# Turning the MLP's input with block transposes and a trip through DRAM instead of on PE, two modulation vectors from 512 KB loads, and a new instruction order, in a planned one-core transformer block

## The chip, the cores and the metric

The kernel runs on one core of one Trainium2 chip. The metric is device time in microseconds of one execution; smaller is better. The engines are PE (matrix multiply; PEld is its weight load), DVE (vector), ACT (activation), POOL (general purpose) and SP, which issues the DMAs here.

## The reference, cut to what matters

`x` has 2048 rows of 512 values. Everything is float32.

```python
mod = (silu(c) @ w_mod).reshape(1, 6, 1, 512)
sa, ca, ga, sb, cb, gb = six rows of mod
h = layernorm(x) * (1 + ca) + sa
x = x + ga * A(h)                # 32 heads of 16, linear attention
h = layernorm(x) * (1 + cb) + sb
x = x + gb * B(h)

def A(x):
    q, k, v = heads of x @ wqkv
    phi(t) = concat(softmax(t @ w_phi), softmax(-(t @ w_phi)))   # per head
    o = phi(q) @ (phi(k).T @ v) / (phi(q) @ sum(phi(k)) + 1e-6)
    return o @ wo

def B(x):
    h = gelu(layernorm(x) @ w1)
    hs = concat of the four quarters of h, shifted by +1, -1, +2, -2 rows
    x1 = x + hs @ w2
    return x1 + gelu(layernorm(x1) @ w3) @ w4     # 512 -> 1376 -> 512
```

## The kernel before

**Precision.** A float32 product that must be exact enough is made of three matmuls in PE's float32r format: every operand is split into a high part, which ACT makes by a copy with rounding, and a low part, which DVE or POOL makes as the difference (`hi_lo`). `three` lists the matmuls high by high, high by low, low by high. An operand that is not split goes through PE as plain float32, and the profile counts each such matmul as two records.

**Stages.** Rows are worked on in 8 chunks of 256 (two tiles of 128).

1. Start: `w_phi` is folded into the K and the Q weights (`load_folded`: each weight is cut into sixteen 128 x 128 blocks, and each block is one matmul of `raw` by a block-diagonal `bd`; four blocks, a row of 128 x 512, make one fold, so there are four folds for K and four for Q). `mod_cols` makes `sa` and `1 + ca` as columns, from two of the six parts of `w_mod`: each part is loaded in four 256 KB pieces, scaled by silu(c) and summed (`acc`), and then summed over partitions by matmuls with one column of ones.
2. K, V and Q for each chunk (`h_chunk`, `k_feat`, `v_feat`, `q_feat`, `kv_add`): the normalised rows are turned by PE transposes (`pt<-const,xn`), scaled and split into `hh`. The Q features are stored to DRAM.
3. Attention output and first half of B for each chunk (`phase_a`, `mix`): Q features come back (`e`), get their denominators on DVE and POOL, DVE turns them in 32 x 32 blocks (`turn`, `pT`), PE multiplies by the key-value matrix (`num`, `pp<-pT,const`), `oT` is multiplied by `wo`, then two layernorms, PE transposes (`pt<-const,n`), `w1`, gelu, the shift, `w2`. The rows `x1` (tile `h`) and `x2` go to DRAM.
4. The MLP for each chunk (`phase_b`): `x1` is loaded (`xl`), normalised to `nb`, turned by eight PE transposes (`pt<-const,nb`), split into two `bH` tiles; `up_pair(j)` makes 256 of the 1376 hidden values (`pa<-bH,w`), gelu and the seven combinations of a fast 2 x 2 block product (`gg`); `down(j)` multiplies them by seven prepared blocks of `w4`; `out` and `d` add the pieces to `gb * x1 + x2` and store. POOL prepares `w4` (`raw`, `tw`, `w`) as stage 3 ends.

**What sets the order.** No instruction is issued where the code stands. Every helper records an `Op` with an engine, a cost, tiles read and written and, for some, alternative engines. `Plan.order` then places them one at a time: on every engine it takes, among the instructions that could start within `BIAS["window"]` ns of the earliest, the one with the lowest `o.prio`, which is its number in the code plus `PRIO[group]`; `PICK` and `BIAS` decide between engines; `CAP` limits how many tiles of a name live at once. The groups are named by `plan.at`: `k3` the keys of tile 3, `q3` its queries, `b2` the MLP of chunk 2, `l4` the input of tile 4 to it, and so on. The result is one fixed sequence for each engine, and each engine works through it strictly in order. All DMAs are issued by SP, and each waits until the one eight before it has landed.

```python
o.prio = o.i + PRIO.get(o.group, 0), o.i
...
s, o = min(((s, o) for s, o in cand if s <= first + window), key=lambda z: z[1].prio)
```

Of the kernel before, what the change touches and what calls it, by code (L numbers as in the profile page):

```python
# [9 lines left out]
FR = mybir.dt.float32r  # L10
AF = mybir.ActivationFunctionType
OP = mybir.AluOpType
# [3 lines left out]
P = 128  # L16
# [19 lines left out]
        "s4": ("ke", "qe", "e", "ez", "pT", "gf", "gg", "bH", "za", "tw"),  # L36
        "s2": ("raw", "mod", "acc", "bd", "xl", "xn", "h", "n", "xb", "xc", "gb", "vv", "kvs", "qt", "sg", "gl", "uu", "nb"),
# [3 lines left out]
CAP = {"acc": 19, "bH": 5, "bd": 5, "const": 71, "dram": 17, "e": 3, "ez": 19, "gb": 19, "gf": 10, "gg": 17, "gl":  # L41
# [4 lines left out]

PRIO = {"b0": -185, "b2": -126, "b3": -374, "b4": -71, "b5": 677, "b7": -111, "d0": 184, "d1": -4, "d2": -248, "d3":
# [25 lines left out]
PICK = {"b0": 1500, "b1": 3000, "b2": -3000, "b3": 3000, "b4": 2000, "b5": -1000, "b6": 1000, "b7": 500, "d0":  # L73
# [1113 lines left out]
```

## Time and profile before

| | before |
|---|---|
| median of 3 runs | 594.35 us (594.02 to 595.15) |
| the profiled execution | 594.79 us, of which its span is 593.0 us |
| PE busy | 568.4 us, 96% of the span |
| DVE, ACT, POOL busy | 417.0, 325.8, 350.1 us |
| HBM traffic | 47.76 MB read, 20.97 MB written |

In rows of the profile, `out<-in` are the program's tile names without their numbers, `x16` is a count of records, and what stands after a bar is the busy time in us, the mean ns of one, and the idle time of the engine just before. A row of the timeline or of the chain of waits has start and length in us. Rows by stretch give for each engine its busy time within the stretch, then the granted share of the PE clock, the share of the DMA engines and GB/s.

### The profile page before, as it was taken

Reading aid. Unit: us, or ns where it says so; the run is one execution under the profiler, and the core shown is the slowest. Engines: PE = TensorE matmul, PEld = TensorE weight load, DVE = VectorE, ACT = ScalarE, POOL = GpSimd, SP = SyncE. Lnnn points to the kernel's source line nnn. Section 1 sums busy time; section 2 is a strip of 40 time slices with the busy share of each in tenths; the row PEclk is TensorE's granted clock in tenths of the full one; section 3 lists DMA queues with packets and bytes.
Section 4 is the critical chain, followed back from the end, with each engine's and each line's share of the span. In section 5 each row is a group of like instructions: output and inputs, shape, how many; then the busy total and the mean of one; then the engine's idle time right before and its main releaser. Section 6 shows DMA issues by size and latency. Waiting matters only on the chain.

```text
span 593.0 us, 11872 instructions
## 1 busy us (share of the span) xinstructions
PE 568.4 (96%) x4548; PEld 512.4 (86%) x4548; DVE 417.0 (70%) x830; ACT 325.8 (55%) x699; POOL 350.1 (59%) x293
## 2 busy tenths in 40 slices
PE   4799999999998799999999999999999999999996
PEld 4588888888887478888888899999999999999996
DVE  5567999697399998898863555568475757556644
ACT  4889986683424575555668755545353435243332
POOL 2779998578998487757859699973321210310031
PEclk9799999999999799999999999999999999999999
DMA  8935524320344435534363532240404040303020
GB/s 278 300 110 177 179 80 166 114 88 2 125 143 170 181 129 178 196 104 172 117 212 107 178 103 90 67 137 25 144 1 143 2 125 1 107 1 107 2 90 37
DMA packets 33865, 69.51 MB, mean 117 GB/s; under 512 B 4144, under 2 KB 4784, under 8 KB 33808
## 3 DMA queue, kind: packets, MB, share of 16 engines
q1 hardware_dynamic: 33808, 68.75, 34.9%
q8 instruction: 36, 0.59, 0.4%
q14 instruction: 21, 0.17, 0.1%
HBM read 47.76 MB, written 20.97 MB: 116 GB/s over the span
## 4 chain that ended last, share of the span: by engine, by line
PE 78%; POOL 7%; DMA 5%; DVE 5%; issue 2%; ACT 2%; SPq 1%; POOLq 0%; DVEq 0%
PE pp L460 52%; PE pa L460 22%; PE pt L469 3%; DMA e<-dram 2%; POOL w L411 2%; POOL raw L411 2%; DMA mod<-in_wmod 2%; PE kva L460 1%; POOL tw L411 1%; DMA raw<-in_w 1%; DVE pp L429 1%; SPq L440 1%; DVE pT L727 1%; POOL ez L411 1%; ACT n L392 1%
## 5 line engine op out<-in xcount | busy, mean ns | idle before, releaser
L460 PE MATMUL pa<-bH,w 128*128 128x256 f32 (+1 forms) x1056 | 130.8, 279 | 0.0
L460 PEld LDWEIGHTS pa<-bH,w 128*128 128x128 f32 (+1 forms) x1056 | 126.0, 186 | 0.2
L460 PE MATMUL pp<-w,gg 128*128 128x256 f32 x840 | 107.6, 280 | 0.6 <-POOL w L411 0.6
L460 PEld LDWEIGHTS pp<-w,gg 128*128 128x128 f32 x840 | 102.7, 188 | 2.0 <-POOL w L411 1.0
L460 PE MATMUL pp<-w,hh 128*128 128x512 f32 x384 | 93.9, 401 | 2.9 <-ACT hh L392 2.9
L460 PEld LDWEIGHTS pp<-w,hh 128*128 128x128 f32 x384 | 72.1, 191 | 19.3 <-ACT hh L392 3.0
L409 DVE TENSOR_TENSOR sg<-sg,pa 128x128 f32<-128x128 f32 x80 | 22.6, 282 | 64.3 <-ACT pa L392 64.3
L411 POOL TENSOR_TENSOR w<-raw,w 128x512 fp32r<-128x512 f32 (+3 forms) x40 | 46.1, 1163 | 20.5 <-ACT w L392 19.1
L460 PE MATMUL pp<-w,oT 128*128 128x512 f32 x192 | 49.4, 407 | 2.5 <-DVE oT L409 1.7
L392 ACT ACTIVATE sg<-pa 128x128 f32<-128x128 f32 x40 | 11.1, 276 | 73.5 <-PE pa L460 70.4
L411 POOL TENSOR_TENSOR xb<-xb,gb 128x512 f32<-128x512 f32 x10 | 13.8, 1382 | 63.5 <-DMA xb<-dram 56.2
L460 PE MATMUL pp<-w,sh 128*128 128x512 f32 x192 | 50.5, 401 | 0.1
L460 PEld LDWEIGHTS pa<-nT,w 128*128 128x128 f32 x384 | 47.4, 188 | 2.5 <-issue 1.2
L460 PE MATMUL pp<-hh,w 128*128 128x256 f32 x384 | 48.9, 285 | 0.0
L460 PE MATMUL pa<-nT,w 128*128 128x256 f32 x384 | 48.7, 283 | 0.0
L460 PEld LDWEIGHTS pp<-hh,w 128*128 128x128 f32 x384 | 46.6, 189 | 2.2 <-issue 1.1
L460 PEld LDWEIGHTS pp<-w,oT 128*128 128x128 f32 x192 | 37.1, 195 | 11.9 <-DVE oT L409 2.5
L392 ACT ACTIVATE gg<-pa 128x384 fp32r<-128x384 f32 x40 | 19.7, 492 | 48.1 <-DVE sg L409 47.2
L411 POOL TENSOR_TENSOR ke<-ke,k 128x1024 f32<-128x1024 f32 x16 | 30.9, 1941 | 21.0 <-DVE k L437 7.2
L411 POOL TENSOR_TENSOR ez<-e,const 128x1024 f32<-128x1024 f32 x16 | 38.2, 2398 | 6.8 <-DMA e<-dram 6.1
L460 PEld LDWEIGHTS pp<-w,sh 128*128 128x128 f32 x192 | 34.2, 188 | 8.8 <-issue 1.6
L535 POOL TENSOR_TENSOR rs<-rs,const 128x1 f32<-128x1 f32 x18 | 10.2, 575 | 51.7 <-DVE rs L421 51.5
(142 smaller groups left out, 1114.3 us busy)
## 6 DMA issues: line engine op xcount, KB each, us to landing
xl<-in_x SPq DMA_DIRECT2D x32, 256.0 KB, 3.5
dram<-qe SPq DMA_DIRECT2D x16, 512.0 KB, 2.9
e<-dram SPq DMA_DIRECT2D x16, 512.0 KB, 4.8
raw<-in_w SPq DMA_DIRECT2D x26, 256.0 KB, 3.4
mod<-in_wmod SPq DMA_DIRECT2D x24, 256.0 KB, 4.6
dram<-xl SPq DMA_DIRECT2D x16, 256.0 KB, 2.0
xc<-dram SPq DMA_DIRECT2D x16, 256.0 KB, 4.7
dram<-h SPq DMA_DIRECT2D x16, 256.0 KB, 2.1
```

What stands on the lines that cost most here:

```text
L392: nc.scalar.activation(o(), i(), func, **kw)
L409: dve = ("DVE", 71 + 1.04 * o.n + 90 * (isps(a) and isps(b)), lambda: nc.vector.tensor_tensor(o(), a(), b(), op=op))
L411: pool = ("Pool", cost, lambda: nc.gpsimd.tensor_tensor(o(), a(), b(), op=op))
L429: nc.vector.scalar_tensor_tensor(o(), a(), get(s), b(), op0=op0, op1=op1, **kw)
L440: plan.op("SP", 475, lambda: nc.sync.dma_start(o(), get(src)), [o], [src] if isinstance(src, V) else [], lat=nbytes / 360., after=after)
L460: nc.tensor.matmul(o(), a(), b(), start=s, stop=e, **kw)
L469: nc.tensor.transpose(o(), i(), ident())
L535: plan.op("Pool", 550, lambda: nc.gpsimd.tensor_tensor(r(), v(), mhalf[:, 0:1](), op=OP.pow), [r], [v, mhalf])
L727: plan.op("DVE", 71 + 1.04 * o.n, lambda: nc.vector.transpose(o(), i()), [o], [i])
```

## The change

- **Start.** The small loads of `c`, of the constants and of `w_phi` are issued by ACT (`load_act`). Three groups of four matmuls of a 128 x 128 tile of ones by itself are put on PE (`warm`). The weights to be folded have tiles of their own (`rk`) and the order takes all eight folds ahead of the first projection.
- **Modulation columns.** The two parts come in four loads of 512 KB that hold both. The first part goes as before. For the second, the raw weights are PE's stationary operand and silu(c) is the single moving column, so that the four pieces are summed in PSUM.
- **MLP input.** `layernorm(..., mixed=True)` writes its result with columns reordered in groups of 32; DVE turns 32 x 32 blocks (`yt`); the tile is stored to a DRAM tile `yd`; four DMAs for each chunk (`load_turned`) load it in 512-byte pieces so that it lies turned in `bL`. ACT copies the high part to `bH`, and DVE or POOL leaves the low part in `bL`. In `up`, the low part is read by PE as 8 pieces of 32 columns that lie 128 columns apart.
- **Order.** `PRIO`, `PICK`, `CAP` and `BIAS` are other numbers throughout, and one rule of the plan's PE clock is altered.

```diff
-CAP = {"acc": 19, "bH": 5, "bd": 5, "const": 71, ...
+CAP = {"acc": 6, "bH": 4, "bL": 13, "bd": 9, "const": 71, ...
-PRIO = {"b0": -185, "b2": -126, "b3": -374, ...
+PRIO = {"b0": -200, "b1": 213, "b2": 706, "b3": 93, ...
-BIAS = {"DVE": 6037, "Pool": 3164, "window": 7, ...
+BIAS = {"DVE": 1908, "Pool": -296, "window": 7, ...
...
-    load(cc, c_d, 2048)
+    load_act(cc, c_d, 2600)
     cst = T("const", [P, 2 * P])
-    load(cst, cst_d, 131072)
+    load_act(cst, cst_d, 3000)
...
+    plan.at("warm")
+    for _ in range(3):
+        p = T("pp", [P, NK, P])
+        mms([(p[:, k, :], ones, ones, True, True) for k in range(NK)], [p], [ones])
...
-    def mod_cols(j):
-        acc = mod_acc(j)
-        p = T("pp", [P, NK])
-        mms([(p[:, k:k + 1], acc[:, k * P:(k + 1) * P], ones[:, 0:1], k == 0, k == NK - 1) for k in range(NK)],
+    def mod_cols():
+
+        acc, p = T("acc"), T("pp", [P, 2, NK])
+        for k in range(NK):
+            raw = T("mod2", [P, 2, D])
+            load(raw, wmod_d[k * P:(k + 1) * P, :2 * D].rearrange("p (j n) -> p j n", j=2), 2 * P * D * 4)
+            if k == 0:
+                act(acc, raw[:, 0, :], scale=sv[:, 0:1], alts=("DVE",))
+            else:
+                stt(acc, raw[:, 0, :], sv[:, k:k + 1], acc, OP.mult, OP.add)
+            mms([(p[:, 1, b:b + 1], raw[:, 1, b * P:(b + 1) * P], sv[:, k:k + 1], k == 0 and b == 0, False)
+                 for b in range(NK)], [p], [raw, sv], skip=True)
+        mms([(p[:, 0, b:b + 1], acc[:, b * P:(b + 1) * P], ones[:, 0:1], False, b == NK - 1) for b in range(NK)],
...
+    def store_rows(dst, t, i):
+        plan.op("SP", 475, lambda: nc.sync.dma_start(dst()[t * P:(t + 1) * P, :], i()), [dst[:, t * P:(t + 1) * P]], [i],
+                lat=P * D * 4 / 360.)
+
+    def load_turned(o, src):
+
+        def fn():
+            for b in range(NK):
+                nc.sync.dma_start(o()[32 * b:32 * (b + 1)].rearrange("p a k j -> p a (k j)"),
+                                  src().rearrange("(a i) (b f) -> b i a f", i=32, b=NK)[b])
+        plan.op("SP", 4 * 475, fn, [o], [src], lat=QB * D * 4 / 360.)
+
     def phase_b(c):
-        bhi, blo = [T("bH", [P, NK, QB], FR) for _ in range(2)]
+        yd = T("dram", [TQ * P, D])
         for t in range(TQ):
             tt_ = c * TQ + t
             plan.at(f"l{tt_}")
-            x1 = T("xl")
+            x1, y = T("xl"), T("yt")
             load(x1, x1_s[tt_], P * D * 4)
-            xn = layernorm(x1, "nb")
-            sl = slice(t * P, (t + 1) * P)
-            to_T(xn, bhi[:, :, sl], blo[:, :, sl])
+            turn(y, layernorm(x1, "nb", True))
+            store_rows(yd, t, y)
+        bhi, blo = T("bH", [P, NK, QB], FR), T("bL", [P, QB // 32, NK, 32], FR)
+        load_turned(blo.f32(), yd)
+        hi = bhi.re("p k (a j) -> p a k j", (NK, QB // 32, 32), j=32)
+        hi.idx = hi.idx.transpose(1, 0, 2)
+        hi_lo(hi, blo, blo.f32(), lo_eng="either")
...
-                items += three(p[:n], w[0][:, k, o:o + n], w[1][:, k, o:o + n], bhi[:, k, :], blo[:, k, :], k == 0, k == NK - 1)
+                wh, wl, h = w[0][:, k, o:o + n], w[1][:, k, o:o + n], bhi[:, k, :]
+                items += [(p[:n], wh, h, k == 0, False), (lo_view(p[:n]), wh, blo[:, :, k, :], False, False),
+                          (p[:n], wl, h, False, k == NK - 1)]
```

**The order at the start, on PE.** Before, from the last transposes of the first chunk's rows `xn` to the first projections; `pp_207` and `pp_221` are the modulation columns, `hh` the input of the projections, `pp_255` the first values and `pp_266` the first keys:

```order
L469 MATMUL pt_197<-const_75,xn_167 128x128
L460 MATMUL pp_207<-const_67,acc_137 128x1 x4
L460 MATMUL pp_221<-const_67,acc_180 128x1 x4
L460 MATMUL pp_255<-w_219,hh_243 128x512
L460 MATMUL pp_255<-w_228,hh_243 128x512
L460 MATMUL pp_255<-w_219,hh_243 128x512
L460 MATMUL pp_266<-w_127,hh_243 128x512
```

Now, the same place; `pp_167` holds both columns, `rk_120` to `rk_141` are the Q weights to be folded, `pp_284` the first values and `pp_294` the first keys:

```order
L473 MATMUL pt_216<-const_73,xn_207 128x128
L464 MATMUL pp_167<-const_123,mod_20_114 128x1 x4
L464 MATMUL pp_167<-const_69,acc_165 128x1 x4
L464 MATMUL pp_236<-bd_118,rk_120 128x128 x4
L464 MATMUL pp_248<-bd_118,rk_126 128x128 x4
L464 MATMUL pp_259<-bd_118,rk_134 128x128 x4
L464 MATMUL pp_274<-bd_118,rk_141 128x128 x4
L464 MATMUL pp_284<-w_257,hh_264 128x512
L464 MATMUL pp_284<-w_266,hh_264 128x512
L464 MATMUL pp_284<-w_257,hh_264 128x512
L464 MATMUL pp_294<-w_139,hh_264 128x512
```

The four Q folds stand between the modulation columns and the first projection; before, they stood as pairs among later projections.

**The order in the MLP stage, on PE.** Before, where a `down` of chunk 5 ends and the next `up_pair` of chunk 6 begins; `nb` is the normalised input of a later tile, `bH_5776` and `bH_5797` are high and low part of the chunk's turned input:

```order
L460 MATMUL pp_5910<-w_4565,gg_6120 128x256
L469 MATMUL pt_6173<-const_75,nb_6141 128x128 x4
L460 MATMUL pa_6186<-bH_5776,w_3446 128x256
L460 MATMUL pa_6186<-bH_5797,w_3446 128x256
L460 MATMUL pa_6186<-bH_5776,w_3456 128x256
```

Now, at the start of an `up_pair`; `bL` is the low part:

```order
L464 MATMUL pa_5912<-bH_5296,w_3447 128x256
L464 MATMUL pa_5912<-bL_5207,w_3447 128x256
L464 MATMUL pa_5912<-bH_5296,w_3456 128x256
L464 MATMUL pa_5912<-bH_5296,w_3447 128x256
L464 MATMUL pa_5912<-bL_5207,w_3447 128x256
```

The `up_pair` has the same 24 matmuls, and no row with `nb` is left on PE.

**The order at the end, on POOL.** Before, the last seven instructions, `xb_6972` and `xb_6988` being the two last output tiles, `uu` sums of accumulators, `xc` the rows of `x2`:

```order
L411 TENSOR_TENSOR xb_6276<-xb_6276,uu_6546 128x512
L411 TENSOR_TENSOR xb_6972<-xb_6972,gb_2464 128x512
L411 TENSOR_TENSOR xb_6972<-xb_6972,xc_6712 128x512
L411 TENSOR_TENSOR xb_6988<-xb_6988,gb_2464 128x512
L411 TENSOR_TENSOR xb_6988<-xb_6988,xc_7027 128x512
L411 TENSOR_TENSOR xb_6972<-xb_6972,uu_7239 128x256
L411 TENSOR_TENSOR xb_6988<-xb_6988,uu_7239 128x512
```

Now, the last output tiles being `xb_7178` and `xb_7200`, `xb_6694` and `xb_6709` those of the chunk before, and `gg_7149`, `gg_7180` halves of what PE needs for its last two `down`:

```order
L412 TENSOR_TENSOR xb_6694<-xb_6694,uu_7122 128x256
L412 TENSOR_TENSOR xb_6709<-xb_6709,uu_7122 128x512
L412 TENSOR_TENSOR gg_7149<-sg_7047,gg_7144 128x512
L412 TENSOR_TENSOR gg_7180<-sg_7091,gg_7167 128x512
L412 TENSOR_TENSOR xb_7178<-xb_7178,gb_1772 128x512
L412 TENSOR_TENSOR xb_7178<-xb_7178,xc_6794 128x512
L412 TENSOR_TENSOR xb_7200<-xb_7200,gb_1772 128x512
L412 TENSOR_TENSOR xb_7200<-xb_7200,xc_7229 128x512
L412 TENSOR_TENSOR xb_7178<-xb_7178,uu_7251 128x256
L412 TENSOR_TENSOR xb_7200<-xb_7200,uu_7251 128x512
```

The chunk before the last is finished only next to the last one, and POOL now makes `gg` halves, which DVE made before (30 of 40 in all; none of 40 before).

More of the change, by code (lines that the diff above doesn't have):

```diff
@@ L35 @@
 KIND = {"s8": ("w", "hh", "oT", "nT", "sh"),
-        "s4": ("ke", "qe", "e", "ez", "pT", "gf", "gg", "bH", "za", "tw"),
-        "s2": ("raw", "mod", "acc", "bd", "xl", "xn", "h", "n", "xb", "xc", "gb", "vv", "kvs", "qt", "sg", "gl", "uu", "nb"),
+        "s4": ("mod2", "ke", "qe", "e", "ez", "pT", "gf", "gg", "bH", "bL", "za", "tw"),
+        "s2": ("raw", "rk", "mod", "acc", "bd", "xl", "xn", "h", "n", "xb", "xc", "gb", "vv", "kvs", "qt", "yt", "sg", "gl", "uu", "nb"),
         "ps": ("pp", "pt", "pa", "kva", "pz"),
@@ L103 @@
 TICK, BUSY = 10240 / 3, 1275 * 1.02
-BIAS = {"DVE": 6037, "Pool": 3164, "window": 7, "ADVE": 3278, "AActivation": 2777, "APool": 3479, "start": 1,
+BIAS = {"DVE": 1908, "Pool": -296, "window": 7, "ADVE": 4366, "AActivation": 4510, "APool": 4957, "start": 1,
         "late": 2, "ln_act": [1, 2, 3, 4, 5, 6, 7], "pair": [0, 1, 2, 3, 4, 5, 6, 7], "qpool": [0, 2, 4, 6, 8, 10,
-        12, 14], "tw": "any", "Activation": 4509}
+        12, 14], "tw": "any", "Activation": 1391}
 class Tl:
@@ L154 @@
 class Op:
-    __slots__ = ("i", "eng", "cost", "lat", "fn", "deps", "succ", "tiles", "prio", "left", "end", "table", "alts", "pref", "kind", "group", "duty", "lock", "rec")
+    __slots__ = ("i", "eng", "cost", "lat", "fn", "deps", "succ", "tiles", "prio", "left", "end", "table", "alts", "pref", "kind", "group", "duty", "lock", "rec", "land")
 class Plan:
@@ L195, in op @@
             o.alts[e] = c, f, e == "Pool" or (bool(k) and k[0])
-        o.kind, o.group, o.duty, o.rec = pref, self.group, duty, rec
+        o.kind, o.group, o.duty, o.rec, o.land = pref, self.group, duty, rec, land
         o.deps, o.succ, o.tiles = {after.i} if after else set(), [], []
@@ L317, in order @@
                     step = min(left / rate, (k + 1) * TICK - end)
-                    ticks[k] = ticks.get(k, 0) + step * rate * o.duty
+                    ticks[k] = ticks.get(k, 0) + step * o.duty
                     end += step
@@ L328, in order @@
                 lanes = lanes[1:] + [end]
+            end += o.land
             done[o.i] = end
@@ L453, in mms @@
             else:
-                cost, rec, duty = cost + 2 * max(56, 4 + 0.8333 * b.n) / tiles, rec + 2, 0.5
+                cost, rec, duty = cost + 2 * max(56 if tiles > 1 else 110, 4 + 0.8333 * b.n) / tiles, rec + 2, 0.5
         def fn():
@@ L511, in mod_acc @@
         return acc
-    def mod_cols(j):
-        acc = mod_acc(j)
-        p = T("pp", [P, NK])
-        mms([(p[:, k:k + 1], acc[:, k * P:(k + 1) * P], ones[:, 0:1], k == 0, k == NK - 1) for k in range(NK)],
+    def mod_cols():
[10 more added lines that the diff above has]
+        mms([(p[:, 0, b:b + 1], acc[:, b * P:(b + 1) * P], ones[:, 0:1], False, b == NK - 1) for b in range(NK)],
             [p], [acc, ones], skip=True)
-        ts(cols[:, j, :], p, float(j), None, OP.add, None)
+        for j in range(2):
+            ts(cols[:, j, :], p[:, j, :], float(j), None, OP.add, None)
     def mod_rows(j, plus, tag="const"):
@@ L543, in layernorm @@
         ts(nm, mv[:, 0:1], rs[:, 0:1], -1.0, OP.mult, OP.mult)
-        xn = T(tag)
-        act(xn, xt, scale=rs[:, 0:1], bias=nm, alts=("DVE",))
+        xn, o = T(tag), None
+        if mixed:
+            xt, o = xt.re("p (k b j) -> p k b j", (NK, NK, 32), k=NK, j=32), xn.re("p (b k j) -> p k b j", (NK, NK, 32), k=NK, j=32)
+        act(o or xn, xt, scale=rs[:, 0:1], bias=nm, alts=("DVE",))
         return xn
@@ L601, in body @@
     wp = T("const", [P, NK, DH])
-    load(wp, wphi_d, 32768)
+    load_act(wp, wphi_d, 3000)
     def make_bd(turned):
@@ L616, in load_folded @@
         for g in range(NK):
-            raw = T("raw")
+            raw = T("rk")
             load(raw, wqk_t[i * D + g * P:i * D + (g + 1) * P, :], P * D * 4)
@@ L646, in body @@
     plan.at("mod")
-    mod_cols(0)
-    mod_cols(1)
+    mod_cols()
     sa, ca1 = cols[:, 0, :], cols[:, 1, :]
```

15 lines of the change are left out of this document (10 added, 5 removed), and 102 rows, old and new, of tables (CAP, PICK, PRIO).

## The prediction

> **What bounds the kernel now.** I read the page's busy line first, then every engine by stage (rows by stretch: start and end, length, then busy us and records of PE, PEld, DVE, ACT, POOL, the granted clock, DMA share, GB/s), and then the timeline where PE is not full.
>
> ```profile
> PE 568.4 (96%) x4548; PEld 512.4 (86%) x4548; DVE 417.0 (70%) x830; ACT 325.8 (55%) x699; POOL 350.1 (59%) x293
> 0.00:20.55 20.55, 8.94 (x56) 8.27 (x56) 11.93 (x31) 10.53 (x20) 5.82 (x14) 0.91 0.90 297
> 20.55:161.40 140.85, 140.85 (x1135) 119.00 (x1139) 106.76 (x162) 104.34 (x213) 116.93 (x77) 0.99 0.38 127
> 161.40:205.60 44.20, 38.04 (x390) 30.20 (x380) 43.06 (x70) 19.41 (x37) 35.45 (x23) 0.92 0.45 161
> 343.50:379.40 35.90, 35.34 (x277) 33.75 (x276) 19.59 (x48) 20.04 (x43) 35.82 (x36) 1.00 0.26 85
> 379.40:584.60 205.20, 205.20 (x1724) 203.29 (x1723) 126.50 (x321) 82.12 (x181) 53.75 (x51) 1.00 0.21 65
> 584.60:593.10 8.50, 3.84 (x27) 3.36 (x25) 3.58 (x8) 1.06 (x3) 1.97 (x2) 0.85 0.17 64
> ```
>
> PE is the bound: it is never idle from 20.55 to 161.40 nor from 379.40 to 584.60. So a matmul that leaves PE there is worth its whole time. PE waits in three places: the start (11.6 us), the transition from the keys to the attention output (6.2 us, where DVE is busy 43.06 of 44.20 us), and the tail. POOL is full from 343.50 to 379.40, where it prepares `w4`.
>
> **The change part by part.** The sum is made against the profiled execution, 594.79 us, whose span is 593.0; the median of the runs shown is 594.35, so it lies 0.44 lower.
>
> *a. Transposes leave PE.*
>
> ```profile
> L469 PE MATMUL pt<-const,nb 128*128 128x128 f32 x64 | 9.3, 272 | 0.0
> 465.98 0.87 PE pt L469 x8
> L460 PE MATMUL pa<-bH,w 128*128 128x256 f32 x960 | 118.1, 279 | 0.0
> ```
>
> The group has 64 records and 9.3 us, but matmuls overlap; the chain of waits shows what a group of eight takes from PE's line: 0.87 us. Eight chunks: 8 x 0.87 = 7.0 us, all in the stretch where PE is full. **-7.0.** What replaces them (DVE turns, a store, four loads, ACT's copy) is on engines that are busy 62% and less there, and the order issues the loads of later chunks several chunks ahead.
>
> *b. Start.* What PE waited for is in these rows: start, length, and in brackets the idle time and its releaser.
>
> ```profile
> 8.25 5.15 DMA mod<-in_wmod
> 14.77 1.53 DVE L429 SCALAR_TENSOR_TENSOR acc<-mod,const,acc 128x512 f32<-128x512 f32 x2
> 16.35 1.26 PE L460 MATMUL pp<-const,acc 128*128 128x1 f32 x8 [1.03 <-DVE acc L429]
> 17.13 0.63 ACT L392 ACTIVATE w<-raw 128x512 fp32r<-128x512 f32 x1 [1.09 <-DMA raw<-in_wv]
> 19.91 1.07 ACT L392 ACTIVATE hh<-pt 128x512 fp32r<-128x512 f32 x2
> 20.55 12.96 PE L460 MATMUL pp<-w,hh 128*128 128x512 f32 x48 [2.94 <-ACT hh L392]
> 0.00:10.00 10.00, 3.65 (x16) 3.49 (x16) 4.03 (x15) 2.59 (x4) 2.75 (x10) 1.00 0.78 248
> 10.00:20.00 10.00, 5.29 (x41) 4.78 (x40) 7.84 (x16) 7.39 (x16) 2.62 (x4) 0.85 1.00 340
> ```
>
> The DMA engines are full from 10 us on. In the new order 3.66 MB stand in the queue up to the last piece of `w_mod` (four `rk` 1.0, two `xl` 0.5, four `mod2` 2.0, small ones). 248 GB/s for 10 us is 2.48 MB, the other 1.18 MB at 340 GB/s take 3.5: 13.5. Then one piece of DVE, a few tiny matmuls and the scaling would give `hh` near 17. But on ACT that `hh` copy stands behind the copy of a V weight whose load is at 4.9 MB: (4.9 - 2.48) / 0.34 = 7.1, so 17.1, and 0.63 for that copy and 0.54 for one `hh` give 18.3. The first projection starts at 18.4 instead of 20.55: **-2.1** (-3.6 to -0.6, by whether the queue or ACT is the later).
>
> *c. Four folds before the first projection.* Between 0 and 20.55 PE has 11.6 us free, and the four Q folds fall into that wait.
>
> ```profile
> 6.35 3.78 PE L460 MATMUL pp<-bd,raw 128*128 128x128 f32 x16 [6.35 <-DVE bd L409]
> 34.38 1.79 PE pp L460 x16
> ```
>
> Two folds (16 records) took 1.79 us inside the full stretch. Four: 2 x 1.79 = **-3.6**. If their loads come late, half of it is lost.
>
> *d. Clock at the start.*
>
> ```profile
> 20.00:30.00 10.00, 9.45 (x34) 7.55 (x35) 5.17 (x10) 8.81 (x21) 8.92 (x8) 0.81 0.84 270
> 101.13 13.79 PE pp L460 x60
> ```
>
> Granted clock 0.81 from 20 to 30. Later, 60 projections took 13.79, 0.230 each; the first 48 took 12.96 instead of 11.0. With PE busy until about 17 and 18.4 the first start, I take **-1.2** (-2.0 to 0). [...]
>
> *e. The transition.*
>
> ```profile
> 190.00:200.00 10.00, 4.93 (x41) 2.62 (x40) 10.00 (x17) 5.36 (x15) 5.14 (x4) 0.73 0.79 281
> 192.50 0.67 PE L460 MATMUL pp<-pT,const 64*32 64x256 f32 x16 [2.23 <-DVE pT L727]
> 197.90 4.16 PE L460 MATMUL pp<-w,oT 128*128 128x512 f32 x10 [1.74 <-DVE oT L409]
> ```
>
> DVE is busy all of it. The DVE instructions between the last key sums and the first `nT`, priced by their rows of before, add to 43.5 us in the new order and 42.9 in the old. PE has 45.5 us of its own work there instead of 40, but most of the added part stands before the first `num`, where nothing waits. So **0** (-6 to +6): -6 would be all of PE's idle time, +6 as much again.
>
> *f to i. Places where POOL or the round trip may be late.*
>
> ```profile
> L411 POOL TENSOR_TENSOR xb<-xb,gb 128x512 f32<-128x512 f32 x10 | 13.8, 1382 | 63.5 <-DMA xb<-dram 56.2 <-ACT gg L392 7.3
> L411 POOL TENSOR_TENSOR xb<-xb,xc 128x512 f32<-128x512 f32 x11 | 14.8, 1349 | 2.4 <-DVE xb L409 1.0 <-DMA xc<-dram 0.7
> L411 POOL TENSOR_TENSOR xb<-xb,uu 128x512 f32<-128x512 f32 x6 | 7.7, 1289 | 0.5 <-DVE nm L421 0.5
> L411 POOL TENSOR_TENSOR xb<-xb,uu 128x256 f32<-128x256 f32 x7 | 5.2, 739 | 38.7 <-DVE uu L409 38.7
> L411 POOL TENSOR_TENSOR w<-tw,w 128x1024 fp32r<-128x1024 f32 x3 | 7.3, 2425 | 0.0
> dram<-xl SPq DMA_DIRECT2D x16, 256.0 KB, 2.0
> xl<-dram SPq DMA_DIRECT2D x16, 256.0 KB, 3.0
> e<-dram SPq DMA_DIRECT2D x16, 512.0 KB, 4.8
> 587.22 1.22 PE L460 MATMUL pp<-w,gg 128*128 128x256 f32 x9
> 589.27 0.69 DVE L409 TENSOR_TENSOR xb<-xb,pp 128x512 f32<-128x512 f32 x1 [0.39 <-POOL xb L411]
> 584.40 1.57 PE L460 MATMUL pp<-w,gg 128*128 128x256 f32 x12
> 585.81 1.57 PE L460 MATMUL pp<-w,gl 96*128 96x512 f32 x6
> ```
>
> - f. At the end of the keys the last sums stand on POOL; it has 27 us of work by its rows against 33 of PE. **+1.0** (0 to +2).
> - g. The first turned chunk: store 2.0, four loads between 3.0 (a 256 KB load) and 4.8 (512 KB) after 1.8 of issuing, ACT's copy 1.1, the difference 1.2 (DVE) to 2.4 (POOL): 9 to 12 us. Between the turn and the first `up` PE has about 12 us of other work: **+0.5** (0 to +4). The loads are in short pieces, which no row of before prices: at twice the 4.8 it is the +4.
> - h. POOL's chain for `w4` is 45 us by its rows from the last `w1` on, and PE's cover, by the order, is longer by 0.4 to 3 us: **+0.5** (0 to +3).
> - i. Tail. Before, PE's last matmul ends at 588.44, DVE's last sum at 589.96, the span at 593.0. Now POOL scales, adds `xc` and adds `uu` for both last tiles after its last half of `gg`: 2 x (1.38 + 1.35) + 0.74 + 1.29 = 7.5 us. PE has 6 matmuls with `gl` (1.57) and 24 with `gg` (0.131 each, 3.1) from about that half to its end. POOL ends 2.8 after PE, and DVE's last sum, 0.69, ends 3.5 after PE instead of 1.5: **+2.0** (0 to +4.2; the lower end if POOL has that half done earlier, the upper if all of its last output work slips by two more of its rows).
>
> Two more table loads of ACT and 17 more DMAs on SP lie in stretches where ACT is busy 64% and less: 0 (0 to +1.5).
>
> Sum: -7.0 - 2.1 - 3.6 - 1.2 + 0 + 1.0 + 0.5 + 0.5 + 2.0 = **-9.9**. 594.79 - 9.9 = 584.9, and 584.4 against the median.
>
> **The rivals.**
>
> *R1, the transition is relieved too.* Rows of e: PE is idle for about 6 us and ran at 0.73 of its clock. If the new order lets other PE work fill both, -8: 584.4 - 8 = **576**. For it: PE has 5.5 us more work there. Against it: DVE's sum is no shorter. Chance 0.10.
>
> *R2, the low part is slow to read (slower).* `up` now reads one operand of three in 8 pieces of 32 columns. That is 8 chunks x 44 = 352 matmuls in the full stretch.
>
> ```profile
> 172.68 1.98 PE L460 MATMUL pp<-acc,const 128*128 128x512 f32 x4
> ```
>
> At half the rate (0.115 us more, half of the 0.230 of 512 columns) they cost 352 x 0.115 = 40 us: 584.4 + 40 = **624**. It breaks even at 9.9 / 352 = 28 ns a matmul. Against it: the `num` matmuls already read 8 pieces of 32 columns, 16 records in 0.67 us; they run several tiles at once, so two rounds of 8, and 256 columns of plain float32 should take half of 1.98 / 4, which is 0.25 a round or 0.50. The row is 0.17 over that, but with start and end in it, and at a slower rate of columns than float32r, so it is not excluded. Chance 0.07, of it 0.06 slower.
>
> *R3, POOL or DVE slips.* POOL gets about 56 us more by its rows, 30 halves of `gg` among it; f, h and i are where PE waits for it. At their far ends they add 2 + 3 + 4.2 - 3.5 = 5.7 to the sum, and e's far end adds 6. Half of the first, or all of both: 584.4 + 2.8 to + 11.7 = **587 to 596**. For it are these rows:
>
> ```profile
> 578.65 0.69 DVE L409 TENSOR_TENSOR gg<-sg,gg 128x512 fp32r<-128x512 f32 x1
> L409 DVE TENSOR_TENSOR gg<-sg,gg 128x512 fp32r<-128x512 f32 x40 | 32.6, 816 | 0.2 <-ACT gg L392 0.2
> ```
>
> DVE took 0.69 while POOL was idle and 0.816 in the mean: they hinder each other. [...] In the middle of stage 4 it costs nothing, as DVE is busy 126.50 of 205.20. Chance 0.14: faster 0.04, same 0.03, slower 0.07.
>
> *R4, every turned chunk comes late.* Eight waits of over 1.2 us eat the gain; at 3 us each, 584.4 + 24 = **608**. The order issues chunk 7's loads before chunk 2's output, which speaks against it. Chance 0.04, of it 0.03 slower.
>
> **How the numbers follow.** The forecast has 0.65. A measurement of this kernel tells about 0.2% (1.2 us) from no change. Faster: 0.65 + 0.10 + 0.01 + 0.04 + 0.01 = 0.81; same 0.03; slower 0.06 + 0.07 + 0.03 = 0.16. The range: the gains that are uncertain (b 1.5, d 0.8, e 6) reach 576, where R1 lies too; the losses f to i and a part of e reach 593. R2, R4 and the upper part of R3 are left out, about 0.2 with the ends.
>
> **What would show it.** Right: no row of `nb` on PE; first `pp<-w,hh` at 18 to 19 and a clock over 0.9 from 20 to 30; `pa<-bL,w` at the mean of `pa<-bH,w`; PE full in stage 4 with no wait for `bL` or `bH`. Wrong: a pitch of `bL` matmuls 28 ns higher (R2), PE waiting for POOL's `w` near the end of stage 3 or a tail over 6 us from PE's last matmul to the end (R3), a wait at every first `up_pair` (R4). A stretch 190 to 203 with PE full would be R1.

## The result and the profile after

The changed kernel took 602.13 us (median of 4 runs, 598.58 to 602.94), before 594.75 on the same chip: the ratio is 1.0114, 95% interval 1.0070 to 1.0157. It is 1.1% longer, clear of the noise, where 584.4 was forecast. Medians, ranges and ratios from here on leave out runs that lie more than 1.5% above the fastest of the same kernel. Its profiled execution took 602.73 us with a span of 601.0.

Stage rows of both kernels, cut at the same points of the work: the first matmul with `oT`, the last with `nT`, PE's last. Columns as in the prediction's stage rows. Before:

```profile
0.00:184.60 184.60, 172.99 (x1484) 147.23 (x1485) 140.96 (x227) 122.20 (x243) 145.95 (x104) 0.98 0.44 147
184.60:341.50 156.90, 149.00 (x1034) 123.08 (x1033) 124.63 (x224) 98.76 (x227) 110.79 (x99) 0.98 0.47 159
341.50:588.44 246.94, 246.38 (x2034) 242.13 (x2032) 150.29 (x380) 104.83 (x229) 92.54 (x92) 1.00 0.22 68
588.44:593.00 4.56, 0.00 (x0) 0.00 (x0) 1.13 (x2) 0.00 (x0) 0.80 (x1) 0.72 0.31 115
```

After:

```profile
PE 577.2 (96%) x4532; PEld 519.1 (86%) x4532; DVE 414.4 (69%) x810; ACT 318.9 (53%) x672; POOL 408.9 (68%) x338
0.00:184.50 184.50, 182.09 (x1532) 156.51 (x1533) 149.16 (x239) 112.48 (x222) 148.17 (x111) 0.98 0.42 147
184.50:340.70 156.20, 148.12 (x1023) 122.74 (x1022) 121.14 (x216) 99.76 (x225) 112.53 (x99) 0.97 0.48 159
340.70:595.13 254.43, 246.94 (x1981) 239.81 (x1979) 141.99 (x354) 106.68 (x225) 146.19 (x128) 1.00 0.33 100
595.13:601.00 5.87, 0.00 (x1) 0.00 (x0) 2.08 (x5) 0.00 (x0) 1.99 (x2) 0.70 0.24 91
```

Up to the attention output nothing is gained in this execution: PE's idle time there fell from 11.6 to 2.4 us, and its busy time rose by 9.1. The second stretch is 0.7 shorter. The third lost 7.5 us: PE has 53 records fewer and is busy 0.6 longer, and it waits 7.5 us where it waited 0.6. The tail lost 1.3.

**The start.** PE, then ACT, in the timeline of after (start, length), then rows by stretch, the last for after over the time of half clock:

```profile
0.99 3.78 PE L464 MATMUL pp<-const 128*128 128x128 f32 x16 [0.99 <-POOL const L489]
6.19 5.81 PE L464 MATMUL pp<-bd,rk 128*128 128x128 f32 x32 [1.42 <-POOL bd L412]
18.65 6.37 PE L464 MATMUL pp<-bd,rk 128*128 128x128 f32 x32
24.77 7.58 PE L464 MATMUL pp<-w,hh 128*128 128x512 f32 x32
20.70 1.07 ACT L393 ACTIVATE hh<-pt 128x512 fp32r<-128x512 f32 x2
10.00:20.00 10.00, 10.00 (x78) 10.00 (x78) 6.09 (x16) 4.71 (x8) 1.07 (x2) 0.86 1.05 395
20.00:30.00 10.00, 10.00 (x51) 9.08 (x50) 6.68 (x12) 8.23 (x23) 7.04 (x8) 0.80 0.65 214
17.20:24.00 6.80, 6.80 (x33) 6.80 (x34) 3.58 (x8) 3.20 (x7) 3.04 (x3) 0.50 0.70 244
```

The same for before, over its time of half clock:

```profile
17.00:23.90 6.90, 3.96 (x12) 3.15 (x12) 2.46 (x5) 6.66 (x17) 5.67 (x6) 0.51 1.03 385
```

From 6.19 on PE never waits. The input `hh` was there from 21.2 on, but PE was at the four Q folds until 24.8, and these 32 records took 6.37 us, 5.35 of it at half clock. Before had half clock for as long, but PE had work for only 3.96 of those 6.90 us; now it had work for all of them.

**The wait in stage 4.** DVE, POOL, SP and PE of after:

```profile
376.03 0.56 DVE L410 TENSOR_TENSOR gg<-pa,gg 128x384 fp32r<-128x384 f32 x1 [4.43 <-POOL w L412]
376.51 5.81 DVE L410 TENSOR_TENSOR gg<-sg,gg 128x512 fp32r<-128x512 f32 x1
382.95 0.68 DVE L410 TENSOR_TENSOR h<-pp,h 128x512 f32<-128x512 f32 x1
375.94 2.02 POOL L412 TENSOR_TENSOR w<-raw,w 128x256 fp32r<-128x256 f32 x2
377.91 2.59 POOL L412 TENSOR_TENSOR w<-tw,w 128x768 fp32r<-128x768 f32 x2
380.44 1.33 POOL L412 TENSOR_TENSOR raw<-raw,gb 128x512 f32<-128x512 f32 x1
387.11 1.29 POOL L412 TENSOR_TENSOR raw<-raw,gb 128x512 f32<-128x512 f32 x1 [5.34 <-DMA raw<-in_w]
383.66 0.33 SPq L448 DMA_DIRECT2D dram<-h  x1
384.08 0.88 SPq L441 DMA_DIRECT2D raw<-in_w  x2
396.71 1.21 PE L464 MATMUL pp<-w,gg 128*128 128x256 f32 x8 [2.52 <-POOL w L412]
```

A DVE operation of 0.69 us (a combination `gg` with both inputs in SBUF) took 5.81. It ends 0.55 after POOL's fifth instruction in a row, at 381.77. Behind it on DVE stood the sum `h`; SP waited for that to store it; behind that store on SP stood a load for `w4`; POOL, then idle, waited 5.34 us for this load; and PE waited 2.52 for POOL's `w`. The DVE operation just ahead, with one input in PSUM (`pa`), took its usual 0.56 while POOL worked.

Not every such meeting ends like this. In the kernel before, an operation of the same form began within a run of POOL instructions too:

```profile
371.40 2.00 POOL L411 TENSOR_TENSOR w<-raw,w 128x256 fp32r<-128x256 f32 x2
372.42 1.52 DVE L409 TENSOR_TENSOR gg<-sg,gg 128x512 fp32r<-128x512 f32 x1
373.35 1.74 POOL L411 TENSOR_TENSOR raw<-raw,gb 128x512 f32<-128x512 f32 x1
```

It waited for one POOL instruction only, which ended at 373.4, and POOL's next one took 1.74 us where such a one took 1.29 in the rows above. None of before's 40 took longer than 1.52.

### The profile page after: what moved, and what is told of

It reads as the page before. It is cut to its first block, busy times and chain, and to the rows that moved or that the text cites. A ratio compares the mean times of both kernels' runs of the same rounds, so it can differ in the third digit from the quotient of the medians.

```text
span 601.0 us, 11985 instructions
## 1 busy us (share of the span) xinstructions
PE 577.2 (96%) x4532; PEld 519.1 (86%) x4532; DVE 414.4 (69%) x810; ACT 318.9 (53%) x672; POOL 408.9 (68%) x338
## 4 chain that ended last, share of the span: by engine, by line
PE 73%; POOL 8%; DMA 6%; issue 4%; ACT 4%; DVE 3%; SPq 1%; POOLq 0%; ACTq 0%; DVEq 0%
PE pp L464 51%; PE pa L464 18%; DMA e<-dram 2%; PE pt L473 2%; POOL ez L412 2%; POOL w L412 2%; PE kva L464 2%; POOL raw L412 1%; DVE xb L410 1%; DMA dram<-yt 1%; ACT n L393 1%; POOL sh L412 1%; POOL tw L412 1%; DVE gg L410 1%; POOL rs L572 1%
## 5 line engine op out<-in xcount | busy, mean ns | idle before, releaser
L464 PEld LDWEIGHTS pa<-bH,w 128*128 128x128 f32 (+1 forms) x704 | 110.2, 187 | 0.0
L464 PE MATMUL pa<-bL,w 128*128 128x256 f32 (+1 forms) x352 | 99.4, 283 | 1.6 <-POOL bL L412 1.6
L464 PEld LDWEIGHTS pp<-w,hh 128*128 128x128 f32 x384 | 70.8, 188 | 15.8
L412 POOL TENSOR_TENSOR gg<-sg,gg 128x512 fp32r<-128x512 f32 x30 | 39.1, 1310 | 53.4 <-DVE gg L410 45.4
L464 PEld LDWEIGHTS pa<-bL,w 128*128 128x128 f32 (+1 forms) x352 | 65.2, 185 | 2.0 <-POOL bL L412 1.8
L412 POOL TENSOR_TENSOR w<-raw,w 128x512 fp32r<-128x512 f32 (+3 forms) x40 | 47.8, 1205 | 17.3 <-ACT w L393 10.0
```

The lines of the kernel that those rows point to most:

```text
L412: pool = ("Pool", cost, lambda: nc.gpsimd.tensor_tensor(o(), a(), b(), op=op))
L464: nc.tensor.matmul(o(), a(), b(), start=s, stop=e, **kw)
```

## The experiments

In most of these kernels the sequence that the plan finds is kept and only the named entries are moved, so the rest of every engine's order stands. The changed kernel itself is not steady: its medians in three sets were 602.1, 601.1 and 598.6, so ratios to before on the same chip are given, and what the traces show. A stretch "from the last `nT` to PE's end" is counted from the start of that matmul; in this measure before has 247.1 us and the changed kernel 254.6.

**The changed kernel again, twice.** No edit.

> The changed kernel once more, nothing edited, so that the edits have something to stand against on the same chip. Its four times so far lie between 598.6 and 602.9 us. Theory A (a DVE operation that is shut out by POOL near 376 us, with what follows from it, is there in some executions and not in others): the times fall into a lower group near 598.5 and an upper one near 602, and a profiled execution near 598.5 has no DVE operation of several us there. Theory B (the spread is in the start's DMA and clock): the profile shows the stall of 5 to 6 us whatever its time.

601.14 us (595.57 to 603.43), ratio 1.0079 (1.0046 to 1.0112). Its profiled execution had the operation at 5.76 us and the first projection at 24.88.

> The changed kernel, nothing edited, to stand beside the next three on their chip: 600 to 604 us by the runs so far.

598.59 us (594.6 to 601.8), ratio 1.0062 (1.0029 to 1.0096). In the profiled execution of this second set too the stall has its full length. With it stand PE's rows, and a row by stretch, to be set against the one from 10 to 20 us above:

```profile
372.97 5.79 DVE L426 TENSOR_TENSOR gg<-sg,gg 128x512 fp32r<-128x512 f32 x1
17.64 3.82 PE L480 MATMUL pp<-bd,rk 128*128 128x128 f32 x32
21.21 1.18 PE L480 MATMUL pp<-w,hh 128*128 128x512 f32 x4
10.00:20.00 10.00, 10.00 (x93) 10.00 (x92) 7.33 (x18) 5.66 (x10) 1.21 (x3) 1.00 1.05 396
```

Here the Q folds ran at full clock, and the first projection came 3.6 us earlier than in the other execution of the same instructions. So theory B holds: the stall is there in each of the seven profiled executions whose stage 4 has this order in DVE, POOL and SP (5.76 to 5.81 us), and the start differs by the clock. Eight profiled executions have the changed kernel's start. Three of them kept full clock from 9.5 us or earlier (this one, and the runs e6 and e8 below): first projection at 19.9 to 21.2, first matmul with `oT` at 179.7 to 181.0, where before had 184.6. Four were at half clock for 6.8 us around 20 us, and one for two times 3.4.

**The load ahead of the store.**

```diff
 SP:  raw (fifth block of w4, first half)
-     dram<-h (last store)
-     raw (fifth block of w4, second half)
+     raw (fifth block of w4, second half)
+     dram<-h (last store)
```

> One swap of neighbours in the order of SP: the second load of raw for the fifth block of w4 is issued ahead of the last store of h, not behind it. Theory A (PE's wait of 2.5 us for POOL's w at 394 us comes from that store: it waited for DVE until 383.7, and the load behind it left POOL idle for 5.3 us): POOL's idle time near 382 to 387 and PE's wait near 394 are gone, 2 to 3.5 us less than the changed kernel. Rival (POOL's chain for w4 is too long anyway, or the next thing is late): PE's wait stays over 1.5 us or turns up elsewhere, under 1 us less.

602.92 us, ratio 1.0120 (1.0094 to 1.0145): nothing gained. POOL and DVE, and PE's wait:

```profile
375.02 2.02 POOL L429 TENSOR_TENSOR w<-raw,w 128x256 fp32r<-128x256 f32 x2
376.98 2.58 POOL L429 TENSOR_TENSOR w<-tw,w 128x768 fp32r<-128x768 f32 x2
379.51 2.52 POOL L429 TENSOR_TENSOR raw<-raw,gb 128x512 f32<-128x512 f32 x2
383.34 0.73 POOL L429 TENSOR_TENSOR tw<-raw,tw 128x256 f32<-128x256 f32 x1
375.58 9.03 DVE L427 TENSOR_TENSOR gg<-sg,gg 128x512 fp32r<-128x512 f32 x1
385.98 0.80 PE L481 MATMUL pp<-w,gg 128*128 128x256 f32 x2 [4.83 <-ACT gg L410]
```

The wait for `w` is gone, but POOL now had no gap until 384.07, and DVE's operation was held for 9.03 us, until 384.6. PE waited 4.83 for what came behind it. The rival's "turns up elsewhere" was right, and it shows the cause: at this place the stall is as long as POOL's unbroken work, and in both cases it ends 0.55 us behind it. The clock was granted at half from 383.4 to 390.2, from within this wait on (0.83 in the mean of 380 to 400).

**The same half of `gg` on POOL.** One entry changes its engine, at its place in the sequence; and once more with the swap above. What the expectations call the lock is that DVE's operation was shut out, 5.81 and 9.03 us, while POOL worked.

```diff
-DVE:  gg<-sg,gg   (chunk 0, the half held for 5.8 us)
+POOL: gg<-sg,gg
```

> One instruction changes its engine: the gg half of chunk 0 that DVE was 5.8 us about near 376 us (0.69 us of work) goes to POOL, at its place in the order. Theory A (that DVE operation, with two inputs in SBUF, was shut out as long as POOL worked without a pause, and with the swap of the two loads on SP it was shut out for 9.0 us because POOL then had no pause: so the lock is the cause, and the store of h, the load of raw, POOL's idle time and PE's waits near 382 and 394 follow from it): no DVE operation over 3 us near 376, h is stored before 379, POOL's gap of 5 us is gone, PE's waits between 380 and 400 fall from 4 to 5 us to under 1.5, and from the last matmul with nT to PE's end the trace is 3 to 4.5 us shorter than the changed kernel's 254.6. Rival (POOL's chain for w4 sets PE's progress in any case, and gets 1.3 us longer by this): that stretch is no shorter, or longer by about 1 us.

598.33 us, ratio 1.0046 (1.0019 to 1.0072). POOL takes 1.29 for it, and has no gap from 380 to 400, while PE is full:

```profile
375.25 1.29 POOL L429 TENSOR_TENSOR gg<-sg,gg 128x512 fp32r<-128x512 f32 x1
380.00:400.00 20.00, 19.97 (x164) 19.53 (x163) 8.29 (x27) 10.73 (x22) 20.00 (x20) 1.00 0.16 54
```

From the last `nT` to PE's end 250.5 us instead of 254.6: theory A. It is below all six traces with this stage as it was (the changed kernel, its two repeats, and the runs e3, e7 and e10: 253.5 to 256.7). The store of `h` came at 379.96, past the 379 expected, because this execution stood about 3 us later as a whole.

> That gg half on POOL, and the swap of the two neighbours on SP (the load of raw ahead of the last store of h). Theory A: the swap has nothing left to mend, as the store of h no longer waits; within 0.7 us of the kernel with the gg half alone on POOL. Rival (the store of h is late for another reason, such as the slot that gg waits for): the swap gains 1.5 us or more on it.

596.99 us, ratio 1.0020 (0.9995 to 1.0045); 250.3 from the last `nT` to PE's end, against 250.5. The trace says that the swap does nothing more; the two intervals overlap.

**The start, three times.** First the four Q folds ahead of the third piece of the modulation columns:

> The four folds of the Q weights stand on PE ahead of the third piece of the modulation columns, not behind the columns. Theory A (hh was ready at 21.2 us and the first projection started at 24.8 because the folds stood in front of it, and took 6.4 us instead of 3.6 since the one-column matmuls had let the clock fall to half): the folds run at 0.112 us a record inside the wait for w_mod, the first projection starts at 21 to 22, and the time is 2.5 to 4 us less than the changed kernel. Rival (the start is bound by the loads, what is gained there is waited for later in K, V and Q): the first projection starts earlier, but the time is within 1 us of the changed kernel.

606.32 us, ratio 1.0172 (1.0145 to 1.0199): both theories missed. These folds did run at full clock (3.65 us), but the columns came that much later, PE then waited 2.6 us for `hh`, and its first projections ran at half clock until 28.0. The folds had no wait to hide in. Then the matmuls of ones and one fold moved:

> The third group of matmuls of ones moves ahead of the first K fold, so that PE has work from 1.0 to about 6.2 us, and the first Q fold moves ahead of the third piece of the modulation columns; the other three folds stay behind the columns. Theory A (from 6.2 us on PE has no free time at the start in the changed kernel, so its time there is its work at the granted clock, and the K folds ran at half of it because the matmuls of ones ended 1.8 us before them): the K folds run at 0.112 us a record, the first projection starts at 20 to 22.5 instead of 24.9, and the time is 2 to 4 us less than the changed kernel. Rival (when the clock rises and falls depends on where an execution begins, not on these 2 us): the K folds are at half clock in the profiled execution all the same and the median is within 1 us.

604.71 us, ratio 1.0127 (1.0087 to 1.0166). The K folds ran at full clock from 7.2 us on, as theory A says, but PE then had nothing to do for 1.7 us near 12 us, the clock was at half from 14.0 to 27.7, and the first projection came at 27.3. Then with this wait filled:

```diff
 PE:  ones x2
+     ones                       (the third group, from further down)
      K folds
      columns, piece 1
-     ones
+     ones                       (new)
      columns, piece 2
+     ones                       (new)
      columns, piece 3;  transposes of xn
+     Q fold 1
      columns, piece 4 and sum
-     Q folds 1 to 4
+     Q folds 2 to 4
```

> The start alone: the third group of matmuls of ones ahead of the K folds, two more such groups between the pieces of the modulation columns, where PE would wait for w_mod, and the first Q fold behind the transposes. Theory A (PE's time from 6 us to the first projection is its work at the granted clock; the run with the start moved showed the K folds at full clock but the clock lost again in a wait of 1.9 us near 12 us; with that wait filled it stays): the Q folds run at 0.112 us a record, the first projection starts at 20 to 22.5 in the profiled execution, where the changed kernel had 24.8 and 24.9, and the median is 2 to 4 us less than the changed kernel, with less spread. Rival (one-column matmuls and transposes let the clock fall whatever stands between them): the Q folds run at 0.213 and the median is within 1 us.

596.06 us, ratio 0.9997 (0.9967 to 1.0026), the changed kernel beside it 1.0062 (1.0029 to 1.0096). PE's rows:

```profile
0.99 4.62 PE L486 MATMUL pp<-const 128*128 128x128 f32 x24 [0.99 <-POOL const L511]
6.58 3.84 PE L486 MATMUL pp<-bd,rk 128*128 128x128 f32 x32 [0.97 <-POOL bd L434]
18.15 2.92 PE L486 MATMUL pp<-bd,rk 128*128 128x128 f32 x24
20.84 0.50 PE L486 MATMUL pp<-w,hh 128*128 128x512 f32 x1
```

The folds are at full clock, the first projection at 20.84: theory A. This one trace does not show it alone, since e6 and e8 had as much without the edit (19.92 and 20.16). But all five traces with this start, here and in the four runs that take it over below, kept full clock from 6.4 us or earlier until the projections, against three of eight without it, and the two intervals lie apart. Its times spread over 590 to 599, so less spread was wrong.

**The low part in plain rows.** The pieces that DMA and DVE leave are written once more into order when the low part is made.

```diff
-    hi_lo(hi, blo, blo.f32(), lo_eng="either")
+    bx = plain tile [P, NK, QB]
+    act(hi, blo.f32());  bx (read as pieces) = blo - hi
...
-    (lo_view(p[:n]), wh, blo[:, :, k, :], False, False)
+    (p[:n], wh, bx[:, k, :], False, False)
```

> The low part of the MLP's turned input is written to a tile of its own in plain rows of 256, so that PE reads it as one run and not as 8 pieces of 32 columns 128 apart; order and number of instructions on every engine as in the changed kernel. Theory A (alternating between a plain and a scattered operand keeps the up matmuls at a pitch of 118 ns, where before had 113 to 114 in long stretches and 115.8 in the mean): the mean pitch of the up matmuls falls to 115 to 116, 2 to 3 us less than the changed kernel. Rival (the pitch goes with the place of weights and accumulators, which the new order set): pitch stays at 118, within 0.5 us.

602.85 us, ratio 1.0127 (1.0097 to 1.0155). The pitch fell as expected: over the stage from 118.2 to 114.8 ns by the records' starts, and the chain of waits shows the same 84 up matmuls at a stretch in the changed kernel

```profile
560.59 9.92 PE pa L464 x84
```

and with plain rows:

```profile
555.48 9.57 PE pa L481 x84
```

But the stage did not get shorter (254.4 in the trace): PE's waits in it were 8.5 us where they had been 7.5, for `gg` and for the low part above all. So the pitch was theory A's, the time the rival's. A kernel in which PE is full shows the price better:

> The kernel before with its low part stored and read in 8 pieces of 32 columns, 128 apart, as in the changed kernel; the order of every engine is that of before, and DVE's difference writes the pieces. Theory A: the pitch of the up matmuls rises from 116.0 to 118 to 119 ns, 1056 x 2.5 = 2.6 us, and as PE is never idle there the time rises by 2 to 3.5 us. Rival (the pitch goes with the places of weights and accumulators in the new order): pitch 116, within 0.7 us of before.

```diff
 # the kernel before, order of every engine unchanged
-    blo = [P, NK, QB], read as one run of 256
+    blo = [P, QB // 32, NK, 32], written by DVE and read by PE in 8 pieces of 32, 128 apart
```

598.54 us, ratio 1.0059 (1.0042 to 1.0075): 3.6 us more than before, and the pitch went from 116.0 to 118.4. In the stage itself the trace shows 2.7 us more (249.8 instead of 247.1); its profiled execution was 1.2 us later at the first projection. The time is a little over theory A's 2 to 3.5.

**All together.** The first try had the poor start in it:

> All of it: the gg half on POOL, the swap on SP, the start of the run above, and the low part in plain rows. Theory A (three separate causes whose shares add: the start 2 to 4, the lock 3 to 4.5, the pitch 3.6 by the profile of the run with plain rows): 8 to 11 us less than the changed kernel, 592 to 595 where that is at 603, and so 2 to 5 below before on this chip. Rival (each gain is waited for elsewhere, as with the swap alone): under 5 us less.

600.47 us, ratio 1.0073 (1.0048 to 1.0097): the rival, since its first projection came at 27.6; the rest of its trace was as in the runs above (251.0). Then stage 4 alone, with the next wait mended:

```diff
 gg half of chunk 0 on POOL, the swap on SP, plain rows, and
-POOL: bL<-bL,bH (chunk 2)
+DVE:  bL<-bL,bH (chunk 2)
 SP:
+     bL<-dram x4 (chunk 2)
      out_dram<-xb (chunk 0), first store
-     bL<-dram x4 (chunk 2)
```

> Stage 4 alone: the gg half on POOL and the swap of the two neighbours on SP as before; the low part of chunk 2 on DVE, not on POOL, and its load ahead of the stores of chunk 0's output; the low part in plain rows. Theory A (with the lock out of the way the next wait is PE's for this low part near 404 to 412, and plain rows pay 3.6 us only where nothing else is late): from the last matmul with nT to PE's end 246 to 248.5 in the profiled execution, where the gg half with the swap had 250.3 and the changed kernel 254.6 to 256.3; 6 to 8 us less than the changed kernel in the median. Rival (POOL and DVE bound the stage's first chunks, plain rows are waited for elsewhere): 249 to 251, 4 to 5.5 us less.

594.96 us, ratio 0.9994 (0.9970 to 1.0018), 246.8 from the last `nT` to PE's end: theory A in the trace. In the median it missed: 3.6 us less than the changed kernel beside it, where 6 to 8 were expected. With the better start:

> The start of the one run and the stage 4 of the other in one kernel. Theory A: the two add, 8 to 12 us less than the changed kernel, and 0 to 5 us below before. Rival (what one gains the other waits for): no more than the better of the two.

592.06 us, ratio 0.9955 (0.9938 to 0.9972): below before, as theory A has it, and better than either alone. The gain on the changed kernel, 6.5 us, is under the 8 to 12 expected. Three runs on one chip then took it apart. Itself:

> The best version so far once more, to stand beside the next ones on their chip: 589 to 595 us, median 591 to 593, 0.2 to 0.7% below before.

591.79 us (591.5 to 593.1), ratio 0.9948 (0.9929 to 0.9966). With the pieces scattered again:

> The best version with the low part scattered as in the changed kernel (8 pieces of 32 columns, 128 apart), nothing else. Theory A (the pieces cost 3.4 ns in each of the 1056 up matmuls, and with the waits gone PE is the bound there): pitch 118 again where plain rows have 114.6 to 115.1, and 2.5 to 4 us more than the best version. Rival (PE's time is not the bound of the stage even there): pitch 118, time within 1 us of the best version.

592.72 us, ratio 0.9961 (0.9945 to 0.9977), pitch 118.2: about 0.9 us, the rival's. The stage was 249.6 instead of 248.0, with fewer waits in it. With 64 transposes put back on PE:

```diff
+    for each chunk, ahead of its first up matmul: eight transposes of a constant tile, read by nobody
```

> The best version with eight PE transposes of a constant tile put in ahead of each chunk's first up matmul, 64 in all, whose result nobody reads: PE gets back the work that the change took from it, and nothing else moves. Theory A (PE is the bound in stage 4, and a matmul that leaves it is worth its pitch, 64 x 0.092 = 5.9 us by the trace of before, not the 7.0 of the forecast): 5 to 7 us more than the best version. Rival (part of it falls into waits of PE): 2 to 4 us more.

599.20 us (597.8 to 599.9), ratio 1.0063 (1.0043 to 1.0082): 7.4 us more, over theory A's 7. All 64 stand behind the last `nT`, and there the trace is 5.9 longer; the other 1.6 us of its difference lie ahead of it, where nothing was edited.

## Why the prediction was wrong, step by step

The forecast missed the profiled execution by 17.8 us. PE's line in the two traces shows where; in stage 4 its records are taken from start to start, with its waits apart (us, after less before, rounded):

| | forecast | measured | difference |
|---|---|---|---|
| to the first `oT` (b, c, d, f) | -5.9 | -0.1 | +5.8 |
| to the last `nT` (e) | 0 | -0.7 | -0.7 |
| from there: transposes (a) | -7.0 | -5.1 | +1.9 |
| PE's waits (g, h) | +1.0 | +6.9 | +5.9 |
| up matmuls (R2, not in the sum) | 0 | +2.5 | +2.5 |
| down matmuls, with `gg` and `gl` | 0 | +2.0 | +2.0 |
| `w2` matmuls of stage 3 (`sh`) that stand behind that point | 0 | +1.2 | +1.2 |
| tail (i) | +2.0 | +1.3 | -0.7 |

- **a, the transposes: right.** Forecast 7.0; put back, they cost 7.4 us of time and 5.9 of the trace. In before's stage 4 stand 56 of them, at 91 ns each from start to start, hence 5.1. In the changed kernel they are gone; their gain was spent on waits.
- **b, c, d, the start: wrong by 5.8 us with f** (forecast -6.9 and +1.0 by 184.5 us, measured -0.1). Step c said that the folds fall into PE's wait. There was no wait left: 40 one-column records stand where 16 stood, with 24 records of ones, and by the rows PE is busy without a gap from 6.19 us on. The time to the first projection is then PE's work at the granted clock.
- **d, the clock, failed most there.** It was taken for a gain of 1.2 us, the author's estimate; no run shows this term. In the profiled execution half clock lasted as long as before (6.8 us in both) and lay over more work: 23 of the 32 Q fold records took 0.213 us from start to start instead of 0.112, as 17 K fold records before 10.2 us had; c's 3.6 us had been priced at full clock. Where the same start kept full clock (c1, e6, e8), the first `oT` came 3.7 to 4.9 us earlier than in before's trace, of the 5.9 forecast. What sets the length of half clock is not shown: it was 6.8 us near the start of before and after, and 13.7 in e7 (14.0 to 27.7). Idle time of PE alone does not explain after, where the clock fell at 17.2 us and PE had not been idle since 6.19.
- **b by itself** had the order on ACT right but the event wrong: `hh` was late because PE's columns were, not for the copy of the V weight. It came at 21.2, not 18.3. With full clock (c1, e6, e8) the first projection was at 19.9 to 21.2, so at most 0.6 of the 2.1 us was there.
- **e: right** (forecast 0; the stretch is 0.7 shorter, with 9 of the 64 transposes of before in it). R1 did not happen: 190 to 200 us stayed as empty as before.
- **h: wrong, the step that failed most in stage 4.** POOL's chain for `w4` was priced +0.5 (0 to +3) from its work and PE's cover. That DVE and POOL hinder each other, as R3 says, was right; the size of it, 0.816 instead of 0.69 us in the mean of before's rows, did not hold: one meeting took 5.1 us of DVE's time. Moving that instruction gave 4.1 us of the trace, and PE's waits in the stage fell from 7.5 to 4.0. The argument that DVE was busy 126.50 of 205.20 in that stage failed, because the sum `h` stood behind that operation in DVE's order and began only at 382.95, and with DVE stood SP, POOL and then PE.
- **R2: right in kind, wrong in size.** Forecast 0 or 115 ns for each of 352 matmuls; measured 2.4 (before's order) to 3.4 ns (plain rows) over all 1056, 2.5 to 3.6 us. Pitch must be read from starts: the groups' mean durations, 279 before and 280 to 283 after, hardly show it.
- **g: in range.** The first turned chunk cost nothing that the waits name in this trace (0.7 us in c1's); the third cost PE 1.6 us, as POOL made its low part.
- **i: right** (forecast +2.0, measured +1.3). POOL's last sum ends 2.1 us after PE (2.8 forecast) and DVE's 2.8 after it (3.5 forecast):

```profile
595.25 1.99 POOL L412 TENSOR_TENSOR xb<-xb,uu 128x256 f32<-128x256 f32 x2 [0.56 <-DVE uu L410]
597.28 0.69 DVE L410 TENSOR_TENSOR xb<-xb,pp 128x512 f32<-128x512 f32 x1 [0.58 <-POOL xb L412]
```

The range reached 593 with the far ends of f, h and i and a part of e's. R3 added them all, to 596. Neither had a term for a start that gains nothing, for slower up and down matmuls, or for one DVE operation held through several of POOL's.

**Open.** Of the 6.9 us that PE waits more in stage 4, the move of one `gg` half to POOL took away 3.4. The other waits are of 0.2 to 1.6 us, for halves of `gg`, for low parts and for `sh`; the mended versions have removed a part (246.8 to 248.0), and they were not told apart one by one. Why the down matmuls are slower (118.3 ns from start to start in before, 120.3 in after) was not tested. Nor is it shown why POOL kept DVE out through five instructions at one place and let it in after one at others. The spread of the changed kernel is explained in part at most. Its start differs by the clock. In six of the eight traces with the stall (all but after and c1) the clock was also at half for 3.4 to 6.9 us between 380 and 407 us; of the eight with that half on POOL only e9 has such a stretch in stage 4, from 413.9. With both places mended, the best version spread over 1.6 us in one set and 6.2 in the other.

## What to carry to other kernels

Price a moved instruction by what it can be held behind, not by its own length: follow its engine's queue to the next store, that store's queue to the next load, and the load to who waits. Before work is put into a bottleneck engine's idle time, add up all that the change puts there, at the clock that it will have. A gain on the bound engine is only seen when nothing else is late: the pieces' 2.4 to 3.4 ns were worth 3.6 us in one order and 0 to 0.9 us in others.

## What the runs showed of the hardware that was not expected

- A DVE operation with two inputs in SBUF can be shut out through a whole run of POOL instructions: one of 0.69 us was held for 5.8 us while POOL ran five in a row, and for 9.0 us while it ran nine. In both traces it ended 0.55 us behind the last of them, so each next instruction of POOL went ahead of it. It is not always so: in before's trace such an operation came in after one POOL instruction (1.52 us). The operation just ahead of the held one, with one input in PSUM, was not held (0.56 us beside POOL).
- PE can be busy without a gap in the profile and lose its clock all the same: the changed kernel's PE shows 10.00 of 10.00 us from 10 to 20 us in two executions, with 0.86 granted in one and 1.00 in the other. With three groups of matmuls of ones ahead of the K folds and two between the columns, instead of two and one, the clock stayed up in five of five traces, against three of eight; that the one-column matmuls are what lets it fall is not shown.
- A low part in 8 pieces of 32 columns, in one of three up matmuls, costs 2 to 3% of their mean pitch (118.4 ns instead of 116.0, 118.2 instead of 114.8), not a multiple of it.
